# Two contraction blocks of three of the last output products moved into the last 20 attention steps, the last softmax sums inverted as columns, and one matmul pair reordered behind each head group

## The chip, the cores and the metric

One core of a Trainium2 chip runs the whole kernel. The metric is the device time of one execution in microseconds (us). Before the change it was 1708.81 us, the median of 3 runs (1708.61 to 1709.07).

## The reference

A transformer block with adaptive layer norm, on x of 2048 rows by 512, 32 heads of 16, and an inner width of 1792:

```python
mod = (silu(c) @ w_mod).reshape(1, 6, 1, -1)      # sa, ca, ga, sb, cb, gb
h = layernorm(x) * (1 + ca) + sa
q, k, v = split(h @ wqkv)                         # 32 heads of 16
o = softmax(q @ k.T * 16 ** -0.5) @ v
x = x + ga * (o @ wo)
h = layernorm(x) * (1 + cb) + sb
x = x + gb * (mish(h @ w1 + b1) @ w2)
```

## The kernel before

Everything is float32. Where a product must be precise and fast, each operand is split into a high part (fp32r, rounded) and a low part, and a product is three matmuls per contraction block of 128: high by high, high by low, low by high. `o_hl` holds the two parts of the attention output of one block of 512 queries, in four contraction blocks k of 128 features (k=0 to 3, eight heads each); the gate `ga` is already multiplied into `wo`.

The queries are cut into 4 blocks (NB) of 512, the heads into 8 groups of 4 (G), so there are 32 pairs of block and group, called n. Each n takes 16 steps; T = 512 steps, and t counts them. Step t works on one half s of the array's rows (rows 64 to 127 in even steps, 0 to 63 in odd ones). Its own work is in the list `mine`: 4 score products (`score`, L527: a matmul of 64 rows into a PSUM bank, then Exp on ScalarE) and, until 20 steps (PRO) before the end, up to 4 products for the row maxima of a later group (`max_tile`, L474: a matmul, then a reduction on VectorE). In the other half of the rows runs `part`, the piece of a background "unit" that this step takes: the MLP and the output projection of the block of queries before, each matmul cut into two halves of 64 rows, the lower half in the even step and the upper half in the odd step (`mm_half`, L131), both adding into one PSUM bank (`ms`). A unit of 12 matmuls takes four steps, six halves a step. `alone` holds maxima products that share the `part` side when `part` is short. At the end of the step comes `pv(t-2)` (L541), the four products of exponentials and values of two steps before, and after the last of a group `evac` (L557), in which ScalarE copies the finished group to `ot` (L563).

Two orderings matter here. First, when a new unit starts (`new`) the step emits one pair ahead of everything: the last own score and the last lone maximum ("early pair", L1230 to L1233), and only then the unit's first matmul, which needs the bank `ms` that ScalarE or VectorE may still be reading. Second, the two halves of the rows may not write one bank at the same time, so the first half-matmul of a step waits until ScalarE has done the exponential of the last score of the step before (`after`, L1226 and L1246); at a new unit this wait is dropped (L1139).

Scores and maxima take PSUM banks from a ring of 6 (`ring`, L150) in the order in which they are emitted: each needs the bank of the sixth before it to have been read.

The last block's own output projection and MLP run after the steps, in `tail` (L983). `tail_loads` (L977) fetches `wo` and the first weights 15 steps before the end; the rows of x to be added are fetched in `tail`. `wo_mms` (L998) makes the four output products, first contraction blocks 0 to 2 and then block 3, which needs the last group. `evac_last` (L605) normalises that group: one matmul with the 0/1 matrix `pick` lays the sums in rows 0 to 63 and the heads in rows 64 to 127 of one bank; VectorE inverts 64 by 512 sums, multiplies, and makes the two parts. Then come the additions to x, the layer norm, and held-back products of the block before (`held`), while TensorE keeps running. All this is one program order per engine, written out by this code.

Of the kernel before, what the change touches and what calls it, by code (L numbers as in the profile page):

```python
# [8 lines left out]
F32 = mybir.dt.float32  # L9
# [9 lines left out]
def adaln_block(ctx: ExitStack, tc: tile.TileContext, x, wqkv, wo, w1, b1, w2, c, w_mod, out):  # L19
    nc = tc.nc  # L20
    P = 128
    S, D = x.shape[1], x.shape[2]
    F = w1.shape[1]
    H = 32
    DH = D // H
    DK = D // P
    FT = F // P
    TB = 512
# [4 lines left out]
    T = 16 * NIT  # L33
# [3 lines left out]
    VROW = NKC * 4 * VW + 16  # L37
    LEAD = 4
    PRO = 16 + LEAD
# [6 lines left out]
    x = x[0]  # L46
# [11 lines left out]
    woscr = dram.tile([DK, P, 2, D], F32, name="woscr")  # L58
# [4 lines left out]
    ident = cst.tile([P, P], F32, name="ident")  # L63
# [20 lines left out]
    gates = [cst.tile([P, D], F32, name=f"gate{i}") for i in range(2)]  # L84
# [43 lines left out]
        acc, l, r, start, stop = m  # L128
        nc.tensor.matmul(acc, l, r, start=start, stop=stop)  # L129

    def mm_half(m, g, after):  # L131


        acc, l, r, start, stop = m
        i = nc.tensor.matmul(acc, l[64 * g:64 * g + 64], r[64 * g:64 * g + 64], start=start and not g, stop=bool(stop and g))  # L135
# [10 lines left out]
    NRING = 6  # L146
    ring_t = ps.tile([P, NRING, TB], F32, name="ring")
    ring_at = [0]

    def ring(w=1):  # L150
        if w == 2 and ring_at[0] % 2:
            ring_at[0] += 1
        b = ring_at[0] % NRING
        ring_at[0] += w
        return ring_t[:, b, :] if w == 1 else ring_t[:, b:b + 2, :]
# [41 lines left out]
    def at(h, f):  # L197

        hooks.setdefault(h, []).append(f)
# [4 lines left out]
    ka = [kq.tile([P, S], F32R, name=f"ka{i}") for i in range(2)]  # L204
# [116 lines left out]
    with ExitStack() as es:  # L321
# [276 lines left out]
    def make_pick():  # L598
# [3 lines left out]
        for i, src in enumerate((cols[:, :, DH:DH + 1].to_broadcast([P, 4, DH]), cols[:, :, :DH])):  # L602
            nc.gpsimd.tensor_copy(pick[:, i, :].rearrange("p (h w) -> p h w", w=DH), src)

    def evac_last(dn):  # L605

        ot, od, rb = mst["last"]
        oh, ol = o_hl[NB - 1]
        r = slice(64, P)
        nc.tensor.matmul(dn, mst["pick"].rearrange("p a w -> p (a w)"), ot, start=True, stop=True)  # L610
        nc.vector.reciprocal(rb[r], dn[:64, :])
        nc.vector.tensor_mul(od[r], dn[r, :], rb[r])
        hi_copy("v", oh[r, DK - 1, :], od[r])
        lo_sub("v", ol[r, DK - 1, :], od[r], oh[r, DK - 1, :])

# [351 lines left out]
    def half_tile(t, j, scr):  # L967

        w = t[:, j * 2 * D:(j + 1) * 2 * D]
        nc.sync.dma_start(w.bitcast(F32), scr.rearrange("p v m -> p (v m)"))  # L970
        return w.rearrange("p (v m) -> p v m", v=2)

    def w1_tail(f):
        i, j = divmod(f % 8, 2)
        return load_w1(f) if i == 1 else half_tile(ka[(1, 0, 2, 3)[i]], j, w1scr[f])

    def tail_loads():  # L977
        for k in range(DK):
            wos[k] = half_tile(ka[(4, 0)[k // 2]], k % 2, woscr[k])
        for f in range(2):  # L980
            w1s[f] = w1_tail(f)

    def tail():  # L983

# [2 lines left out]
        y, xn = [], []  # L987
        for v in (y, xn):
            for i in range(4):
                v.append(ap.tile([P, D], F32, tag=f"p{i}", name="y", bufs=3 + i % 2))  # L990
        for i in range(4):
# [6 lines left out]
        def wo_mms(i, ks):  # L998
            s = slice(i * P, (i + 1) * P)
            seq = [(l, r, k) for l, r in ((oh, 0), (oh, 1), (ol, 0)) for k in ks]  # L1000
            for j, (l, r, k) in enumerate(seq):
                nc.tensor.matmul(accs4[i], l[:, k, s], wos[k][:, r, :], start=(k == 0 and j == 0),
                                 stop=(k == 3 and j == 2))

        norms = []
        wo_mms(0, (0, 1, 2))
        evac_last(ring())
        wo_mms(1, (0, 1, 2))
        for i in (2, 3):
            accs4[i] = bank("ring")  # L1010
            wo_mms(i, (0, 1, 2))
        for i in range(4):
            wo_mms(i, (3,))
            nc.vector.tensor_add(y[i], accs4[i], y[i])
# [159 lines left out]
    def step(t):  # L1174
        second = t % 2
        n, u = t // 16, t % 16 // 2
        tm = t + PRO
        run_hooks(2 * t)
        if t < 0:

            for i in range(2):
                if tm < 16:
                    kb, jq = divmod(2 * tm + i, 8)
                else:
                    jq, kb = tm % 16 // 2, 2 * second + i
                max_pair(tm // 16, jq, kb)
            if second and tm % 16 == 15:
                neg_max(tm // 16)
            run_hooks(2 * t + 1)
            for f in ats.pop(t, []):  # L1190
                f()
            whole_units(2 * t + 1, CREDIT)
            do_specials(2 * t + 1)
            return
        s = 0 if second else 1
        own, others = ([score(n, j, v, 2 * u + i) for i in range(2) for j in range(2)] for v in (s, 1 - s))
        if not second and 1 < t < T:
            next_part(2 * t)
        part = list(cur["part"])
        f = len(part)  # L1200
        if t >= T:
            if t == T:
                cur["tag"] = "acc"
            run_hooks(2 * t + 1)
            pv(t - 2)
            whole_units(2 * t + 1, 8)
            do_specials(2 * t + 1)
            return
        if tm < T:
            o = max(0, (8 - f) // 2)  # L1210
            mo, alone = maxima(tm // 16, tm % 16 // 2, s, o)

            mine = [x for p in zip(mo, own) for x in p] + own[len(mo):]
        else:
            o = max(0, (4 - f) // 2)
            mine = own[o:] if second else own[:4 - o]
            alone = others[4 - o:] if second else others[:o]

            m = len(mine)
            if f > m:  # L1220
                mine = [mine[(i * m) // f] if (i + 1) * m // f > i * m // f else None for i in range(f)]
        beside = part + alone

        def emit(product):
            e = product()
            if e is not None and cur.pop("want", None):  # L1226
                cur["after"] = e

        mid = False
        if cur.pop("new", None) and alone and len(mine) > f:  # L1230

            emit(mine.pop())
            emit(beside.pop())  # L1233
        for i in range(max(len(mine), len(beside))):
            if i == len(mine) // 2:
                run_hooks(2 * t + 1)

            if not f and tm < T and i == (2 if mst.get("norming") else 3):
                pv(t - 2)
                mid = True  # L1240
            if i < f:
                last = i + 1 == f
                if i < len(mine) and mine[i] and not last:
                    emit(mine[i])
                for m in beside[i]:
                    mm_half(m, second, cur.pop("after", None))  # L1246
                if last:
                    cur["want"] = True
                    if i < len(mine):
                        emit(mine[i])  # L1250
                    if second and not cur["left"]:
                        cur["fin"](2 * t + 2)
                        cur["fin"] = None
            else:
                for x in (*mine[i:i + 1], *beside[i:i + 1]):
# [147 lines left out]
```

## Time and profile before

| | us |
|---|---|
| median of the runs | 1708.81 |
| the profiled execution | 1705.6 |
| its span (first to last instruction) | 1703.8 |
| the last 19 steps (from 1548.82 until the last values products at 1598.19) | 49.37 |
| the last three values products | 2.71 |
| `tail` until output block 3 can start | 9.34 |
| from there to the end | 93.56 |

The profiled execution took 1.8 us more than its span, and the median of the runs is 3.2 us above it. A timeline row gives the start in us from the beginning of the span, the length in us, the engine, the line in the listing, the operation, the tile written and the tiles read, the shape, and how many instructions were merged; in brackets is the idle time before it and what ended that. A window row gives a stretch, its length, and for each engine the busy time and number of instructions in it, then the granted TensorE clock, the DMA share and GB/s. A float32 matmul shows as two instructions. Busy rows of TensorE overlap, since matmuls are pipelined: what counts is the distance from one start to the next.

### The profile page before, as it was taken

The page shows a single profiled execution, that of the slowest core. Times are in us where ns is not written, and L with a number is a line of the kernel's source. Part 1 is how long each engine was busy: PE and PEld are TensorE (multiplying, and loading weights), DVE is VectorE, ACT ScalarE, POOL GpSimd, SP SyncE. Part 2 cuts the span into 40 slices and gives each one's busy share as a digit, 9 for nine tenths or more (in the row PEclk, how much of TensorE's full clock was granted, in tenths as well). Part 3 has the DMA queues.
Part 4 walks back from the last instruction along what each step waited for, and adds up shares of the span by engine and source line. Part 5 has one row for each costly group of instructions (what it writes and reads, how often), then busy time and mean ns, then how long its engine had stood idle before and what let it go on. Part 6 is the DMA issues. An engine that isn't in the chain of part 4 may idle for free.

```text
span 1703.8 us, 33660 instructions
## 1 busy us (share of the span) xinstructions
PE 1675.0 (98%) x12372; PEld 915.5 (54%) x12372; DVE 1437.6 (84%) x2368; ACT 1356.9 (80%) x2613; POOL 807.6 (47%) x829
## 2 busy tenths in 40 slices
PE   7999999999999999999999999999999999999999
PEld 5755665555445455555555455555545445554587
DVE  6888888888889888888889898888889888883377
ACT  6257777777778988888888998888878988888574
POOL 5155224665413464655423564556323654555442
PEclk9999999999999999999999999999999999999999
DMA  7777457777773342434355433424354433424261
GB/s 253 187 235 214 109 162 216 237 234 222 234 208 101 99 109 76 134 80 126 83 151 148 118 74 94 139 76 126 88 143 124 124 93 83 137 68 157 84 228 63
DMA packets 113997, 240.08 MB, mean 141 GB/s; under 512 B 24048, under 2 KB 49648, under 8 KB 107784
## 3 DMA queue, kind: packets, MB, share of 16 engines
q1 hardware_dynamic: 113832, 237.92, 48.6%
q8 instruction: 98, 1.61, 0.4%
q14 instruction: 67, 0.55, 0.1%
HBM read 179.95 MB, written 51.44 MB: 136 GB/s over the span
## 4 chain that ended last, share of the span: by engine, by line
PE 84%; DMA 5%; ACT 4%; DVE 4%; issue 1%; SPq 0%; POOL 0%; ACTq 0%; DVEq 0%; POOLq 0%
PE bk L549 26%; PE ring L531 20%; PE ring L482 18%; PE bk L135 10%; PE bk L129 4%; DVE mx L484 3%; ACT pr L534 3%; PE ring L1110 2%; PE ring L129 2%; DMA qa<-mt 1%; DMA ka<-kscr 1%; PE ring L496 1%; DMA w<-woscr 1%; ACT hb L722 1%; PE ring L843 0%
## 5 line engine op out<-in xcount | busy, mean ns | idle before, releaser
L484 DVE TENSOR_REDUCE mx<-ring 128x1 f32<-128x512 f32 x1968 | 1222.0, 681 | 159.9 <-PE ring L482 142.1
L534 ACT ACTIVATE pr<-ring 128x512 f32<-128x512 f32 x2048 | 1078.2, 602 | 217.8 <-PE bk L135 128.1
L482 PE MATMUL ring<-ka,qa 64*128 64x512 f32 x1968 | 815.7, 429 | 5.2 <-ACT pr L534 3.5
L531 PE MATMUL ring<-qa,ka 64*128 64x512 f32 x2048 | 759.2, 403 | 6.5 <-DMA qa<-mt 3.7
L549 PE MATMUL bk<-pr,vg 128*32 128x512 f32 x4096 | 545.1, 604 | 0.0
L482 PEld LDWEIGHTS ring<-ka,qa 64*128 64x128 f32 x1968 | 349.1, 184 | 321.6 <-DVE mx L484 230.2
L531 PEld LDWEIGHTS ring<-qa,ka 64*128 64x128 f32 x2048 | 373.5, 184 | 200.2 <-DVE mx L484 129.8
L135 PE MATMUL bk<-h,w 64*128 64x512 f32 (+1 forms) x1080 | 279.6, 391 | 0.1
L135 PE MATMUL bk<-w,a_h 64*128 64x512 f32 x632 | 211.6, 413 | 0.3 <-ACT pr L534 0.2
L135 PEld LDWEIGHTS bk<-h,w 64*128 64x128 f32 x1080 | 178.5, 184 | 13.0 <-ACT pr L534 4.3
L549 PEld LDWEIGHTS bk<-pr,vg 128*32 128x32 f32 x4096 | 80.8, 108 | 137.7 <-issue 126.4
L135 PE MATMUL bk<-w,a_l 64*128 64x512 f32 x316 | 124.0, 392 | 0.0
L135 PEld LDWEIGHTS bk<-w,a_h 64*128 64x128 f32 x632 | 107.5, 184 | 16.9 <-ACT pr L534 8.3
L899 POOL TENSOR_TENSOR y<-yd,y 128x512 f32<-128x512 f32 x44 | 56.8, 1292 | 90.5 <-ACT yd L898 85.3
L734 POOL TENSOR_SCALAR qq<-ee 128x512 f32<-128x512 f32 x25 | 15.5, 619 | 171.5 <-ACT ee L728 171.5
L750 POOL TENSOR_TENSOR qq<-qq,rr 128x512 f32<-128x512 f32 x42 | 54.2, 1289 | 83.8 <-ACT rr L744 83.6
L736 POOL TENSOR_TENSOR hb<-hb,ee 128x512 f32<-128x512 f32 x42 | 54.1, 1287 | 82.7 <-DVE ee L732 80.7
L135 PE MATMUL bk<-w,o_hl 64*128 64x512 f32 x288 | 79.2, 404 | 0.0
L98 POOL TENSOR_TENSOR a_l<-hb,a_h 128x512 fp32r<-128x512 f32 x53 | 72.0, 1358 | 4.4
L135 PEld LDWEIGHTS bk<-w,a_l 64*128 64x128 f32 x316 | 58.3, 184 | 4.9
L135 PE MATMUL bk<-h_h,wl 64*128 64x512 f32 x168 | 57.1, 420 | 0.0
L752 POOL TENSOR_TENSOR rr<-rr,qq 128x512 f32<-128x512 f32 x42 | 54.1, 1287 | 3.5
(189 smaller groups left out, 1841.5 us busy)
## 6 DMA issues: line engine op xcount, KB each, us to landing
ka<-kscr SPq DMA_DIRECT2D x124, 384.0 KB
w<-w2scr SPq DMA_DIRECT2D x56, 512.0 KB
w<-w1scr SPq DMA_DIRECT2D x46, 512.0 KB
vg<-vscr SPq DMA_DIRECT2D x32, 552.0 KB
qa<-qscr SPq DMA_DIRECT2D x124, 100.0 KB
kscr<-qh SPq DMA_DIRECT2D x16, 512.0 KB
qscr<-qh SPq DMA_DIRECT2D x32, 256.0 KB
hl<-in_B_w SPq DMA_DIRECT2D x28, 256.0 KB
```

Source lines behind the costliest of these rows:

```text
L98: (nc.gpsimd if eng == "p" else nc.vector).tensor_sub(lo, src, hi.bitcast(F32))
L129: nc.tensor.matmul(acc, l, r, start=start, stop=stop)
L135: i = nc.tensor.matmul(acc, l[64 * g:64 * g + 64], r[64 * g:64 * g + 64], start=start and not g, stop=bool(stop and g))
L482: nc.tensor.matmul(pm, qt[64 * s:64 * s + 64, qs * P:(qs + 1) * P], kt[64 * s:64 * s + 64, kb * TB:(kb + 1) * TB], start=True, stop=True)
L484: nc.vector.tensor_reduce(out=mxs[n][:, s, 4 * j + qs, kb:kb + 1], in_=pm, op=ALU.max, axis=AX.X)
L531: nc.tensor.matmul(p_, kt[64 * s:64 * s + 64, kc * P:(kc + 1) * P], qt[64 * s:64 * s + 64, :], start=True, stop=True)
L534: e = nc.scalar.activation(pr, p_, AF.Exp, scale=SCALE)
L549: nc.tensor.matmul(accs[n][32 * h:32 * h + 32, :], vgs[n][:, o:o + 32], pts.pop((t, h)), start=(kc == 0), stop=(kc == 15))
L736: (nc.vector if tail else nc.gpsimd).tensor_mul(hb, hb, ee)
L750: nc.gpsimd.tensor_mul(qq, qq, rr)
L752: nc.gpsimd.tensor_mul(rr, rr, qq)
L899: nc.gpsimd.tensor_add(y[i], yd, y[i])
```

## The change

1. In the steps t = 494 to 511, two more half-matmuls go into `mine` of each step, at its third and fifth place (`first_part`): the six matmuls of contraction blocks 0 and 1 for the first three of the four output products, so 18 matmuls, each as two halves, an upper half in the even step and a lower half in the odd step. They add up in the ring's sixth bank, which is taken out of the ring from step 492 (`kept`); every sixth step VectorE adds the bank to the rows of x in `ys`. `tail` then multiplies block 2 alone for these three products. While such a product is unfinished, a new unit keeps the wait on the exponential.
2. Loads move: two blocks of `wo` to step 483 and two row tiles of x to step 484, ahead in the sync engine's queue of a w1 load, the transfers of a group's sums, the last values load, three w2 loads and the row maxima's transfers; the third row tile of x moves to step 500. The row tiles lie in the gates' buffers and in a free values buffer.
3. The last group's sums: four matmuls of `ot` with four columns of the identity give them as 128 by 16, VectorE inverts these and copies them out to 128 by 256, the heads come with the `pick` matmul and are copied by ScalarE, and four matmuls with the identity turn the inverses back into rows 64 to 127, by which VectorE multiplies.
4. There is no early pair in the steps t with t % 16 = 2. The unit's first matmul then follows the first of `mine`, and the last score and the lone maximum come at the end of the step. This applies to 18 steps: 18, 34, 130, 162 to 274 (every 16th), 386 to 482 (every 16th).

```diff
     def ring(w=1):
         if w == 2 and ring_at[0] % 2:
+            ring_at[0] += 1
+        if kept and ring_at[0] % NRING == NRING - 1:
             ring_at[0] += 1
...
+    def sums_last(cs):
+        ot = mst["last"][0]
+        for q in range(4):
+            nc.tensor.matmul(cs[:, 4 * q:4 * q + 4], ot[:, q * P:(q + 1) * P], ident[:, DH::32], start=True, stop=True)
+        rc = ap.tile([P, 16], F32, tag="rc", name="rc", bufs=2)
+        nc.vector.reciprocal(rc, cs[:, :16])
+        wide = ap.tile([P, TB], F32, tag="p0", name="wide", bufs=3)[:, :256].rearrange("p (q h d) -> p q h d", q=4, h=4)
+        mst["rc"] = wide
+        nc.vector.tensor_copy(wide, rc.rearrange("p (q h) -> p q h", h=4)[:, :, :, None].to_broadcast([P, 4, 4, DH]))
+
+    def heads_last(dn):
+        ot, od, _ = mst["last"]
+        nc.tensor.matmul(dn, mst["pick"].rearrange("p a w -> p (a w)"), ot, start=True, stop=True)
+        nc.scalar.copy(od[64:], dn[64:, :])
+
     def evac_last(dn):
-        ot, od, rb = mst["last"]
+        od, rc = mst["last"][1], mst["rc"]
...
-        nc.tensor.matmul(dn, mst["pick"].rearrange("p a w -> p (a w)"), ot, start=True, stop=True)
-        nc.vector.reciprocal(rb[r], dn[:64, :])
-        nc.vector.tensor_mul(od[r], dn[r, :], rb[r])
+        for q in range(4):
+            nc.tensor.matmul(dn[64:, q * P:(q + 1) * P], rc[:, q].rearrange("p h w -> p (h w)"), ident, start=True, stop=True)
+        nc.vector.tensor_mul(od[r], dn[r, :], od[r])
...
+    def first_part(h):
+        u = first_of
+        if not u["left"] and u["next"] < FIRST:
+            i = u["next"]
+            u["next"] += 1
+            oh, ol = o_hl[last]
+            acc = ring_t[:, NRING - 1, :]
+            s = slice(i * P, (i + 1) * P)
+            seq = [(l[:, k, s], wos[k][:, v, :]) for l, v in ((oh, 0), (oh, 1), (ol, 0)) for k in range(2)]
+            u["left"] = [[(acc, l, r, j == 0, j == len(seq) - 1)] for j, (l, r) in enumerate(seq)]
+            u["fin"] = lambda: nc.vector.tensor_add(ys[i], acc, ys[i])
+        u["part"], u["left"] = u["left"][:2], u["left"][2:]
...
-        wo_mms(0, (0, 1, 2))
+        kept.clear()
+        wo_mms(0, (2,))
+        sums_last(ring())
+        heads_last(ring())
         evac_last(ring())
-        wo_mms(1, (0, 1, 2))
+        wo_mms(1, (2,))
         for i in (2, 3):
             accs4[i] = bank("ring")
-            wo_mms(i, (0, 1, 2))
+            wo_mms(i, (2,) if i < FIRST else (0, 1, 2))
...
-            cur.pop("after", None)
+            if not first_of["left"]:
+                cur.pop("after", None)
...
+            if first_of["part"]:
...
+                for i, slot in enumerate(first_of["part"]):
+                    mine.insert(2 + 2 * i, lambda slot=slot: [mm_half(m, 1 - second, None, second) for m in slot] and None)
...
-        if cur.pop("new", None) and alone and len(mine) > f:
+        if cur.pop("new", None) and alone and len(mine) > f and t % 16 != 2:
             emit(mine.pop())
             emit(beside.pop())
...
+        if second and first_of["part"] and not first_of["left"]:
+            first_of["fin"]()
...
+    at(2 * (T - 29), lambda: load_wos((0, 1)))
+    at(2 * (T - 28), lambda: load_ys((0, 1)))
+    at(2 * (T - 12), lambda: load_ys((2,)))
     at(2 * T - 30, tail_loads)
```

More of the change, by code (lines that the diff above doesn't have):

```diff
@@ L129, in mm_go, with mm_half @@
         nc.tensor.matmul(acc, l, r, start=start, stop=stop)
-    def mm_half(m, g, after):
+    def mm_half(m, g, after, then=None):
         acc, l, r, start, stop = m
-        i = nc.tensor.matmul(acc, l[64 * g:64 * g + 64], r[64 * g:64 * g + 64], start=start and not g, stop=bool(stop and g))
+        then = g if then is None else then
+        i = nc.tensor.matmul(acc, l[64 * g:64 * g + 64], r[64 * g:64 * g + 64], start=start and not then, stop=bool(stop and then))
         if after is not None:
@@ L148, in adaln_block @@
     ring_at = [0]
+    kept = []
     def ring(w=1):
         if w == 2 and ring_at[0] % 2:
+            ring_at[0] += 1
+        if kept and ring_at[0] % NRING == NRING - 1:
             ring_at[0] += 1
@@ L975, in w1_tail, with load_wos, load_ys @@
         return load_w1(f) if i == 1 else half_tile(ka[(1, 0, 2, 3)[i]], j, w1scr[f])
+    FIRST = 3
+    first_of = {"left": [], "fin": None, "part": [], "next": 0}
+    ys = {}
+    def load_wos(ks):
+        for k in ks:
+            wos[k] = half_tile(ka[(4, 0)[k // 2]], k % 2, woscr[k])
+    def load_ys(js):
+        for i in js:
+            ys[i] = gates[i] if i < 2 else ap.tile([P, VROW], F32, tag="vg", name="vg", bufs=2)[:, :D]
+            r = 4 * last + i
+            nc.sync.dma_start(ys[i], x[r * P:(r + 1) * P, :])
     def tail_loads():
-        for k in range(DK):
-            wos[k] = half_tile(ka[(4, 0)[k // 2]], k % 2, woscr[k])
+        load_wos((2, 3))
         for f in range(2):
             w1s[f] = w1_tail(f)
+    def first_part(h):
[10 more added lines that the diff above has]
+        u["part"], u["left"] = u["left"][:2], u["left"][2:]
     def tail():
@@ L989, in tail @@
             for i in range(4):
-                v.append(ap.tile([P, D], F32, tag=f"p{i}", name="y", bufs=3 + i % 2))
-        for i in range(4):
+                v.append(ys[i] if v is y and i < FIRST else ap.tile([P, D], F32, tag=f"p{i}", name="y", bufs=3 + i % 2))
+        for i in range(FIRST, 4):
             r = 4 * last + i
@@ L1001, in wo_mms @@
             for j, (l, r, k) in enumerate(seq):
-                nc.tensor.matmul(accs4[i], l[:, k, s], wos[k][:, r, :], start=(k == 0 and j == 0),
+                nc.tensor.matmul(accs4[i], l[:, k, s], wos[k][:, r, :], start=(k != 3 and j == 0),
                                  stop=(k == 3 and j == 2))
         norms = []
-        wo_mms(0, (0, 1, 2))
+        kept.clear()
+        wo_mms(0, (2,))
+        sums_last(ring())
+        heads_last(ring())
         evac_last(ring())
-        wo_mms(1, (0, 1, 2))
+        wo_mms(1, (2,))
         for i in (2, 3):
             accs4[i] = bank("ring")
-            wo_mms(i, (0, 1, 2))
+            wo_mms(i, (2,) if i < FIRST else (0, 1, 2))
         for i in range(4):
@@ L1199, in step @@
         part = list(cur["part"])
+        if not second:
+            first_of["part"] = []
+            if t == T - PRO:
+                kept.append(NRING - 1)
+            elif T - PRO < t < T:
+                first_part(2 * t)
         f = len(part)
@@ L1217, in step @@
             alone = others[4 - o:] if second else others[:o]
+            if first_of["part"]:
+                assert f
+                for i, slot in enumerate(first_of["part"]):
+                    mine.insert(2 + 2 * i, lambda slot=slot: [mm_half(m, 1 - second, None, second) for m in slot] and None)
             m = len(mine)
```

## The prediction

> **What bounds the kernel now.** I read the page first: the share of each engine, then the chain of work that ended last.
>
> ```profile
> span 1703.8 us, 33660 instructions
> PE 1675.0 (98%) x12372; PEld 915.5 (54%) x12372; DVE 1437.6 (84%) x2368; ACT 1356.9 (80%) x2613; POOL 807.6 (47%) x829
> PE 84%; DMA 5%; ACT 4%; DVE 4%; issue 1%; SPq 0%; POOL 0%; ACTq 0%; DVEq 0%; POOLq 0%
> ```
>
> TensorE sets the time over nearly the whole span, so an edit counts by the distance between TensorE's starts that it removes or adds. Three places are touched: the 18 steps that lose their early pair, the last 20 steps, and the tail. Their stretches, cut by windows (columns: length; PE, PEld, DVE, ACT, POOL busy), first the last steps, the tail up to output block 3, and what follows:
>
> ```profile
> 1548.82:1598.19 49.37, 48.98 (x335) 22.75 (x334) 5.46 (x9) 43.53 (x85) 28.06 (x27) 1.00 0.27 92
> 1600.90:1610.24 9.34, 9.34 (x43) 7.26 (x39) 5.16 (x4) 0.59 (x1) 0.00 (x0) 1.00 0.91 336
> 1610.24:1640.00 29.76, 29.76 (x162) 25.50 (x161) 20.46 (x32) 18.32 (x30) 11.42 (x20) 1.00 0.62 238
> ```
>
> TensorE is never idle in the tail, so matmuls taken out of it shorten it one for one, as long as nothing else becomes late. Then the 18 steps, each from one values product's start to the next: one of the usual kind, the mildest, the one with the most in it, and the sum over all 18. Below them step 322, at the same place in its group but in the middle of a unit and so without an early pair, and the sum over the 18 steps that follow the 18.
>
> ```profile
> 628.01:631.27 3.26, 3.09 (x23) 1.34 (x22) 2.81 (x5) 3.26 (x8) 2.80 (x3) 1.00 0.88 194
> 1377.98:1380.98 3.00, 3.00 (x25) 1.33 (x23) 2.75 (x6) 3.00 (x7) 1.29 (x1) 1.00 0.01 3
> 1279.58:1283.38 3.80, 3.61 (x28) 2.04 (x26) 3.80 (x8) 3.48 (x7) 0.29 (x1) 1.00 0.05 7
> sum 59.48, PE 56.36 PEld 26.20 DVE 52.77 ACT 59.01 POOL 18.66; mean PE 3.13 PEld 1.46 DVE 2.93 ACT 3.28 POOL 1.04
> 1003.57:1006.40 2.83, 2.83 (x24) 1.52 (x23) 2.47 (x5) 2.67 (x7) 2.67 (x3) 1.00 0.12 17
> sum 51.51, PE 51.51 PEld 28.35 DVE 39.73 ACT 40.71 POOL 19.17; mean PE 2.86 PEld 1.57 DVE 2.21 ACT 2.26 POOL 1.06
> ```
>
> The 18 steps average 59.48 / 18 = 3.30 us, the step without an early pair 2.83: the excess is 18 x 0.47 = 8.5 us. ScalarE is busy for 59.0 of the 59.5 us there, but only 40.7 of 51.5 in the steps after, so it catches up at once.
>
> **The early pair: what the stall is.** One of the 18, step 178, in the timeline, TensorE and then ScalarE:
>
> ```profile
> 629.01 0.72 PE L482 MATMUL ring<-ka,qa 64*128 64x512 f32 x2
> 629.35 0.39 PE L135 MATMUL bk<-w,a_h 64*128 64x512 f32 x1
> ...
> 630.05 0.39 PE L135 MATMUL bk<-w,a_h 64*128 64x512 f32 x1
> ...
> 630.61 0.50 PE L482 MATMUL ring<-ka,qa 64*128 64x512 f32 x1 [0.17 <-ACT pr L534]
> ...
> 631.27 0.64 PE L549 MATMUL bk<-pr,vg 128*32 128x512 f32 x4
> ...
> 628.40 0.68 ACT L722 ACTIVATE hb<-bk,b1c 128x512 f32<-128x512 f32 x1
> 628.97 0.60 ACT L534 ACTIVATE pr<-ring 128x512 f32<-128x512 f32 x1
> 629.45 0.61 ACT L563 COPY ot<-bk 128x512 f32<-128x512 f32 x1
> 629.91 1.62 ACT L534 ACTIVATE pr<-ring 128x512 f32<-128x512 f32 x3
> ```
>
> In these steps ScalarE takes the unit's bank (L722, or a copy) and `ot` between two steps' exponentials. The early score's exponential can therefore start only at 629.91 and is over at about 630.55 (it is the first of three that overlap in 1.62). The ring has six banks, so the sixth product after the early score, the third maximum, needs its bank: it should start at 630.28, one slot of 0.23 us after 630.05, and starts at 630.61. With the restart (0.33 us to the next start, as from 629.01 to 629.35, instead of 0.23) the step loses 0.42 us against 2.84.
>
> Without the early pair all products of the step stand two places earlier in the ring. The third maximum then needs the bank of the last step's final score, read by 629.57: no wait. Two waits are left. The unit's first matmul comes in the first slot, 629.01, and needs the bank that L722 reads until 629.08: about 0.13 us with the semaphore. The lone maximum in the last slot, about 630.63, needs the first score's exponential, which now starts no earlier than 629.91 and ends near 630.63: about 0.05. So step 178 would come to 3.02 and gain 0.24. The same working by each step's own rows: 13 of the 18 gain 0.24 to 0.32, in sum 3.4; three mild ones like 1377.98 gain 0.11 each, 0.3. In the last two, the one at 1279.58 and one like it, transposes of the layer norm make the step long, and the copy that the unit waits for is VectorE's and late, which the early pair had covered: I put them at -0.2 together. Sum 3.5 us. Bounds: nothing, if the stall returns at the unit's first matmul; all of the excess, 8.5 less 0.9 for the two steps' transposes (two times four at 0.11, below), 7.6, if all 18 fall to 2.84. A value below the middle is right because the waits that remain are ScalarE's, whose work is not less.
>
> **The tail.** TensorE, then VectorE's chain for the last group, with ScalarE's copy that starts it:
>
> ```profile
> 1600.90 2.36 PE L1002 MATMUL bk<-ka,o_hl 128*128 128x512 f32 x9
> 1603.10 1.02 PE L610 MATMUL ring<-ot,pick 128*128 128x512 f32 x2
> 1603.56 2.66 PE L1002 MATMUL bk<-ka,o_hl 128*128 128x512 f32 x9
> 1606.05 4.35 PE L1002 MATMUL ring<-ka,o_hl 128*128 128x512 f32 x18
> ...
> 1604.16 3.35 DVE L611 RECIPROCAL rb<-ring 64x512 f32<-64x512 f32 x1 [5.10 <-PE ring L610]
> 1607.55 0.69 DVE L612 TENSOR_TENSOR od<-ring,rb 64x512 f32<-64x512 f32 x1
> 1608.28 0.42 DVE L93 CAST o_hl<-od 64x512 fp32r<-64x512 f32 x1
> 1608.73 0.69 DVE L98 TENSOR_TENSOR o_hl<-od,o_hl 64x512 fp32r<-64x512 f32 x1
> ...
> 1601.04 0.59 ACT L563 COPY ot<-bk 128x512 f32<-128x512 f32 x1 [1.77 <-PE bk L549]
> ```
>
> Of 36 matmuls before output block 3, 18 go: the x18 row takes 1610.24 - 1606.05 = 4.19 us, 0.233 each, so 4.19 us less. What is added has no row here; the nearest are
>
> ```profile
> 1603.26 0.86 PE ring L610 x2
> 1617.35 0.87 PE ring L1035 x8
> ...
> L399 PE MATMUL bk<-sel,row 128*128 128x1 f32 x16 | 3.6, 353 | 0.0
> L584 DVE RECIPROCAL rc<-sm 128x16 f32<-128x16 f32 x31 | 7.5, 241 | 0.0
> ```
>
> from the chain of waits and the groups by shape. Turning the inverses back is four float32 products of 128 columns, together as many columns as the one L610: 0.86. The four for the sums are eight instructions that load 128 weights each, like the transposes of L1035 (0.87 for 8): 0.87, where L399, with one column each, shows that few columns don't make them much cheaper. Bounds for the two: 0.4 each (one pass instead of two) and 1.4 to 2.8 each if each instruction takes the 0.18 to 0.35 us of L399's rows, which ran in the first 15 us. Two changes of the array's shape, into 64 columns and back, cost a restart each: 0.1 (0.33 instead of 0.23, as above). So the stretch becomes 9.34 - 4.19 + 0.86 + 0.87 + 0.2 = 7.1, 2.2 us less; by the bounds, between 3.4 less and 0.5 more, and I keep 2.2, since the added products use the same operands as L610 and L1035.
>
> What could be late instead: the sums start when `ot` is there (1601.7), by then three matmuls are done (1601.6). Sums until 1602.6, inversion 0.24, copy to 256 columns about 0.4 (half of a 0.69 row), ready at 1603.4, when TensorE has finished the `pick` product. Products with the identity until 1604.4, then 0.69, 0.42 and 0.69 on VectorE: both parts at 1606.4. TensorE reaches output block 3 at 1608.0, so 1.6 us of other output products cover it; ScalarE's copy of the heads (0.6) ends 1604.2. Everything behind block 3 follows in the same order, fully busy, and moves with it.
>
> A rule that speaks against the added products: the Trainium skill, "TensorEngine Tiling (Array Packing)", section Key Properties, says that a change of tiling mode drains TensorE. The first slot after each values product, 0.33 instead of 0.23, agrees with a small drain, and the sum has it. The same page, Instruction Overhead, gives about 60 cycles to a matmul of few columns, by which (an estimate) the sums would take 0.2 us and the total be 0.7 us better; the rows of L399 do not look like that.
>
> **The last 20 steps.** Two steps, TensorE at the values products and at their ends, then ScalarE:
>
> ```profile
> 1571.76 1.06 PE L549 MATMUL bk<-pr,vg 128*32 128x512 f32 x8
> 1572.75 0.49 PE L135 MATMUL bk<-w,a_h 64*128 64x512 f32 x1
> ...
> 1574.34 1.06 PE L549 MATMUL bk<-pr,vg 128*32 128x512 f32 x8
> 1575.41 0.50 PE L135 MATMUL bk<-w,a_h 64*128 64x512 f32 x1
> ...
> 1573.29 2.06 ACT L534 ACTIVATE pr<-ring 128x512 f32<-128x512 f32 x4 [0.44 <-PE ring L531]
> 1582.56 0.69 DVE L898 COPY yd<-bk 128x512 f32<-128x512 f32 x1 [3.15 <-PE bk L135]
> ```
>
> A step has six half-matmuls of the unit in one half of the rows, and four scores in the other: two slots are free. The two new halves fill them, and I cost them at nothing; the cover is the unit's six slots of 0.23. Without it, 36 x 0.233 = 8.4 us. The fifth bank is enough: a score then needs the fifth before it, whose exponential (four in 2.06 us, done at 1575.35, before the next step starts) is always over. The wait kept at new units costs 1.07 - 0.99 = 0.08, in three steps (498, 502, 510): 0.2. VectorE's addition (0.69) stands behind a unit's copy at one place only, from 1582.56 to about 1583.95, just when the next product wants the bank: 0.1. Against this, the first score now stands ahead of the waiting matmul and starts its exponential up to 0.08 earlier; I take 0.1. Sum: +0.2, from -0.5 to +8.4. The moved loads are seven issues on a queue that has time (DMA share 0.27 above), at least four steps ahead of the sums' transfers behind them: nothing.
>
> **Sum.** -3.5 - 2.2 + 0.2 = -5.5. The span 1703.8 becomes 1698.3, the profiled run 1705.6 becomes 1700.1, and the median, 3.2 above the profiled run, 1708.8 - 5.5 = 1703.3.
>
> **The rivals.**
> - The stall only moves: the unit's first matmul, or the next step, takes what the third maximum lost, since ScalarE's work in the 18 steps is not less (59.0 of 59.5). Against it: 40.7 of 51.5 in the step after. Only the tail is left: -2.0, 1706.8.
> - All 18 steps return to 2.84, since a step without early pair does so although it has `ot` too. For it the 2.83 row; against it that row has one ScalarE instruction less (x7). -7.6 - 2.0: 1699.2.
> - The small products cost more, and with them TensorE waits for VectorE: 1.5 us more in the tail, -4.0: 1704.8.
> - Slower: the new halves are not covered, because both halves of the rows cannot run full with three accumulating banks. Place: the 18 steps from 494; price up to 8.4, -5.7 + 8.4: 1711.5; it decides from 5.7 us, two thirds of the halves, on. Against it: ordinary steps run eight slots with both halves full at 0.23 a slot.
>
> **How the numbers follow.** A change under 0.2% (3.4 us, beyond 1705.4 to 1712.2) cannot be told from none. Forecast 0.55, all returned 0.1, dearer products 0.1: these are faster, and so 0.75. The moved stall 0.17 is within, and most of the slower case (0.08): 0.21 within, 0.04 slower. The range takes in the moved stall and nearly all of the other gain: 1699.6 to 1707.0.
>
> **What would show it.** Right: L482's waits for ScalarE gone from the 18 steps, their sum near 56; the last steps' stretch still near 49.4; output block 3 7.1 us after the last values product; VectorE's inversion at 0.24. Wrong: the sum still near 59, a first matmul of a unit that starts 0.3 late, last steps over 2.7 each, or TensorE idle before block 3.

## The result, and the profile after

The changed kernel takes 1701.47 us (median of 8 runs, 1698.15 to 1704.48) against 1708.09 for the kernel before (median of 8, 1704.94 to 1709.07; the three runs told at the start are among them). The ratio is 0.9965, with a 95% interval from 0.9954 to 0.9976: 4.1 to 7.9 us faster. The page of the kernel after:

```profile
span 1702.7 us, 33730 instructions
PE 1674.4 (98%) x12406; PEld 921.7 (54%) x12406; DVE 1438.2 (84%) x2372; ACT 1359.4 (80%) x2614; POOL 809.3 (48%) x829
PE 90%; DVE 3%; DMA 3%; ACT 2%; issue 1%; SPq 0%; POOL 0%; ACTq 0%; DVEq 0%; POOLq 0%
```

TensorE still sets the time (busy for 98% of the span, 90% of the chain of work that ended last). The span is only 1.1 us shorter than before: the profiled execution is the slowest of the eight (1704.48, 3.0 above their median), and that of before (1705.6) is 2.5 below its median. So the stages have to be read one by one. In the windows of the kernel after, the last steps and the tail, cut at the same instructions as before:

```profile
1550.08:1599.01 48.93, 48.93 (x371) 25.03 (x370) 6.75 (x11) 43.33 (x85) 28.18 (x27) 1.00 0.24 77
1601.73:1609.07 7.34, 7.34 (x41) 5.45 (x38) 2.36 (x5) 1.17 (x2) 0.00 (x0) 1.00 0.93 340
```

and the 18 steps without their early pair: step 178, the sum over the 18, and the sum over the 18 steps behind them:

```profile
631.70:634.73 3.03, 3.03 (x24) 1.81 (x23) 2.61 (x5) 3.03 (x8) 2.85 (x3) 1.00 0.90 196
sum 55.90, PE 55.45 PEld 32.49 DVE 49.80 ACT 55.15 POOL 18.13; mean PE 3.08 PEld 1.81 DVE 2.77 ACT 3.06 POOL 1.01
sum 51.45, PE 51.45 PEld 28.39 DVE 42.69 ACT 45.04 POOL 18.45; mean PE 2.86 PEld 1.58 DVE 2.37 ACT 2.50 POOL 1.03
```

The 18 steps went from 59.48 to 55.90 (3.6 us), the tail from 9.34 to 7.34 (2.0), the last steps from 49.37 to 48.93 (0.4): 6.0 us together. The steps behind the 18 did not grow (51.51 before). From 1609.07 to the end of the span it is 93.6 us, as before.

Some 4.9 us of this are missing from the profiled span. Most of them lie in the first third, where TensorE waits for transfers. Six steps there, 80, 81, 96, 112, 132 and 133, in the windows before, their sum:

```profile
sum 21.84, PE 17.50 PEld 9.01 DVE 14.99 ACT 14.95 POOL 11.51; mean PE 2.92 PEld 1.50 DVE 2.50 ACT 2.49 POOL 1.92
```

and after, with the steps 80, 81 and 133 by themselves:

```profile
337.27:342.76 5.49, 3.51 (x23) 1.78 (x22) 3.02 (x6) 3.17 (x7) 4.31 (x5) 0.87 0.84 245
342.76:346.57 3.81, 3.81 (x24) 1.67 (x22) 1.94 (x4) 1.67 (x4) 3.56 (x5) 0.74 0.93 206
...
496.12:500.04 3.92, 3.92 (x24) 1.77 (x22) 1.86 (x5) 1.67 (x4) 0.00 (x0) 0.71 0.09 12
sum 26.10, PE 21.03 PEld 9.88 DVE 15.05 ACT 15.38 POOL 14.42; mean PE 3.50 PEld 1.65 DVE 2.51 ACT 2.56 POOL 2.40
```

26.10 - 21.84 = 4.3 us. The third number from the end of a row is the granted clock: it fell to 0.71 to 0.87 in these rows. Over the profiles of all the kernels below, the same six steps take 19.5 to 26.1 us, whichever part of the change is in (23.2 for the kernel after once more, e11_after_again), and two others, 108 and 128, vary by 4.3 and 1.4 us. So this changes from execution to execution, and the spans of single profiles can't be compared as they stand.

**What the changed step looks like.** Step 178 after, TensorE, then ScalarE, in the timeline:

```profile
632.70 0.50 PE L487 MATMUL ring<-ka,qa 64*128 64x512 f32 x1
632.83 0.49 PE L136 MATMUL bk<-w,a_h 64*128 64x512 f32 x1
...
633.51 0.39 PE L536 MATMUL ring<-qa,ka 64*128 64x512 f32 x1
...
633.74 0.38 PE L487 MATMUL ring<-ka,qa 64*128 64x512 f32 x1
...
634.32 0.47 PE L487 MATMUL ring<-ka,qa 64*128 64x512 f32 x1
634.73 0.64 PE L554 MATMUL bk<-pr,vg 128*32 128x512 f32 x4
...
632.08 0.69 ACT L744 ACTIVATE hb<-bk,b1c 128x512 f32<-128x512 f32 x1
```

The unit's first matmul waits 0.13 us for L744's bank (632.83 instead of 632.70), the third maximum comes a slot of 0.23 behind the product before it (633.74), the lone maximum last (634.32), and the step ends 3.03 us after it began.

**What the new tail looks like.** TensorE and VectorE between the last group's `ot` and both parts of it:

```profile
1602.54 1.02 PE L614 MATMUL ring<-ident,ot 128*128 128x4 f32 x8
...
1603.42 1.10 PE L624 MATMUL ring<-ot,pick 128*128 128x512 f32 x2
1603.65 0.26 DVE L616 RECIPROCAL rc<-ring 128x16 f32<-128x16 f32 x1 [3.17 <-issue]
1603.94 0.29 DVE L619 COPY wide<-rc 128x256 f32<-128x256 f32 x1
...
1604.45 1.09 PE L633 MATMUL ring<-ident,wide 128*64 128x128 f32 x8
...
1605.47 0.97 PE L1051 MATMUL bk<-ka,o_hl 128*128 128x512 f32 x3
...
1606.82 0.69 DVE L98 TENSOR_TENSOR o_hl<-od,o_hl 64x512 fp32r<-64x512 f32 x1
```

From start to start the sums take 1603.42 - 1602.54 = 0.88 us, the heads 1.03, the inverses turned back 1605.47 - 1604.45 = 1.02. Both parts are there at 1607.51, and TensorE reaches output block 3 at 1609.07 without having stood still.

### The profile page after: what moved, and what is told of

It is laid out like the page before. It is cut to its first block, busy times and chain, and to the rows that moved or that the text cites. A ratio compares the mean times of both kernels' runs of the same rounds, so it can differ in the third digit from the quotient of the medians.

```text
span 1702.7 us, 33730 instructions
## 1 busy us (share of the span) xinstructions
PE 1674.4 (98%) x12406; PEld 921.7 (54%) x12406; DVE 1438.2 (84%) x2372; ACT 1359.4 (80%) x2614; POOL 809.3 (48%) x829
## 4 chain that ended last, share of the span: by engine, by line
PE 90%; DVE 3%; DMA 3%; ACT 2%; issue 1%; SPq 0%; POOL 0%; ACTq 0%; DVEq 0%; POOLq 0%
PE bk L554 28%; PE ring L536 22%; PE ring L487 19%; PE bk L136 10%; PE bk L129 3%; PE ring L1162 2%; PE ring L129 2%; DVE mx L489 2%; ACT pr L539 1%; DMA qa<-mt 1%; DMA xt<-in_A_x 1%; PE ring L501 1%; DMA w<-w1scr 1%; DMA w<-woscr 1%; PE ring L865 0%
```

## The experiments

All times are us. "18 steps" is their sum; "493 to 510" the stretch between the starts of two values products, without the last of the steps; "to block 3" is from the last values product to the start of output block 3, and beside it how long block 3 takes. These four are from the trace of each kernel. The first row is the profile of before.

| kernel | ratio to before (95%) | 18 steps | 493 to 510 | to block 3, block 3 |
|---|---|---|---|---|
| before | 1 | 59.48 | 47.92 | 9.33, 2.78 |
| after | 0.9965 (0.9954 to 0.9976) | 55.89 | 47.56 | 7.34, 2.78 |
| e1_pair_only | 0.9978 (0.9968 to 0.9988) | 55.97 | 47.92 | 9.33, 2.78 |
| e2_columns_only | 1.0013 (1.0002 to 1.0024) | 59.43 | 47.92 | 11.45, 2.77 |
| e3_rows | 0.9958 (0.9944 to 0.9973) | 55.97 | 47.54 | 6.58, 3.18 |
| e4_no_halves | 0.9964 (0.9948 to 0.9980) | 55.88 | 47.48 | 7.34, 2.78 |
| e5_two_maxima | 1.0002 (0.9992 to 1.0011) | 60.93 | 47.53 | 7.33, 2.80 |
| e6_two_maxima_all | 1.0267 (1.0253 to 1.0280) | 60.70 | 47.55 | 7.33, 2.80 |
| e7_rows_low_last | 0.9962 (0.9950 to 0.9974) | 55.88 | 47.55 | 6.58, 2.86 |
| e8_four_banks | one run, 1700.78 | 55.95 | 47.43 | 7.33, 2.80 |
| e9_no_pair | 0.9983 (0.9971 to 0.9995) | 55.75 | 47.55 | 7.34, 2.78 |
| e10_pair_where_it_helps | 0.9970 (0.9957 to 0.9983) | 55.76 | 47.83 | 6.58, 2.87 |
| e11_after_again | 0.9966 (0.9955 to 0.9978) | 55.91 | 47.55 | 7.33, 2.80 |

**The pair alone** (e1_pair_only: the kernel before with this one line of the change):

```diff
-        if cur.pop("new", None) and alone and len(mine) > f:
+        if cur.pop("new", None) and alone and len(mine) > f and t % 16 != 2:
```

> The kernel before with one edit: no early pair in the 18 steps with t % 16 = 2. My theory: the stall at the third maximum is the early score's ring bank, so the 18 steps alone come to 55.9 us in sum (59.5 before), everything else stays, and the time is 3.6 us below the kernel before. Rival one: the shortening of those steps needs the rest of the change or is given back in the steps behind, then the sum or the steps behind stay as they were in total and the time is that of the kernel before (0 +- 1). Rival two: the tail carries the whole 6 us, with the same reading.

The median was 1703.64 against 1707.32, 3.7 us. In its windows the sums over the 18 steps and over the 18 behind them are

```profile
sum 55.98, PE 55.53 PEld 32.61 DVE 49.91 ACT 55.25 POOL 18.04; mean PE 3.09 PEld 1.81 DVE 2.77 ACT 3.07 POOL 1.00
sum 51.52, PE 51.52 PEld 28.39 DVE 42.63 ACT 44.99 POOL 18.44; mean PE 2.86 PEld 1.58 DVE 2.37 ACT 2.50 POOL 1.02
```

so the line is worth 3.5 us by itself, and nothing of it comes back in the steps behind: ScalarE's busy time there rose from 40.7 to 45.0 of 51.5, into time that it had free.

**The columns alone** (e2_columns_only: the kernel before with part 3 of the change, the last group's sums inverted as columns, and all 36 matmuls still ahead of block 3):

```diff
...
+        sums_last(ring())
+        heads_last(ring())
         evac_last(ring())
```

> The kernel before with the last sums inverted as columns and nothing else. My theory: TensorE is never idle there, so the eight small products are paid in full (0.9 and 1.0 us): output block 3 starts 11.3 us after the last values product instead of 9.34, and the time is 2.0 us above the kernel before, although VectorE's inversion falls from 3.35 to 0.26 us. Rival: block 3 waits for VectorE's chain, then the shorter inversion pays for the products, the stretch is 9.3 or less and the time 0 to 1 us below.

```profile
1606.20:1617.65 11.45, 11.45 (x59) 8.93 (x55) 2.36 (x5) 1.17 (x2) 0.00 (x0) 1.00 0.81 299
```

TensorE is busy all of it, and it is 2.1 us longer than before's 9.34: the columns cost TensorE 2.1 us, and save VectorE 2.8 (5.16 busy before, 2.36 here) that no one waits for in this arrangement. By the ratio the whole kernel is 2.2 us slower than before (0.3 to 4.1).

**The halves with the old inversion** (e3_rows: the kernel after with `evac_last` of the kernel before):

```diff
...
-        sums_last(ring())
-        heads_last(ring())
         evac_last(ring())
```

> The changed kernel with the inversion in rows as before (one product with pick, 64 by 512 inverted). Rival, by which the columns are needed: with 18 matmuls gone TensorE waits for the inversion in rows longer than the columns cost, and block 3 starts later than the 7.34 us of the changed kernel (8 or more). My theory: the pick product ends 1.7 us after the last values product, the inversion (3.35), the product (0.69) and the high part (0.42) end at 6.3, the low part at 7.0; TensorE, done at 5.1, waits about 1.2 us for the high part and 0.2 for the low one, so block 3 is through 0.5 to 0.9 us earlier than in the changed kernel, and the time is 0.5 to 0.9 us lower.

The windows until block 3 starts, and of block 3:

```profile
1600.23:1606.81 6.58, 5.39 (x24) 3.63 (x21) 4.54 (x4) 0.59 (x1) 0.00 (x0) 1.00 0.92 322
1606.81:1609.99 3.18, 3.11 (x12) 2.26 (x13) 2.45 (x5) 0.00 (x0) 0.17 (x1) 1.00 0.40 162
```

and VectorE's chain:

```profile
1602.17 3.35 DVE L616 RECIPROCAL rb<-ring 64x512 f32<-64x512 f32 x1 [3.19 <-PE ring L615]
...
1606.28 0.42 DVE L93 CAST o_hl<-od 64x512 fp32r<-64x512 f32 x1
1606.74 0.69 DVE L98 TENSOR_TENSOR o_hl<-od,o_hl 64x512 fp32r<-64x512 f32 x1
```

Now TensorE does wait (5.39 busy of 6.58), until the high part is there at 1606.70, and block 3 takes 0.4 longer because its third matmul needs the low part, ready at 1607.43. Even so block 3 ends 9.76 after the last values product instead of 10.12. The waits, 1.2 us before block 3 and 0.4 in it, are cheaper than the 2.1 us of products that avoid them.

**The same, with the low parts last** (e7_rows_low_last: e3_rows, and in block 3 the high terms of the first two output products ahead of the first low term):

```diff
...
+        wo_high(0)
+        wo_high(1)
         for i in range(4):
-            wo_mms(i, (3,))
+            if i > 1:
+                wo_high(i)
+            wo_low(i)
             nc.vector.tensor_add(y[i], accs4[i], y[i])
```

> The changed kernel with the inversion in rows, and in output block 3 the high terms of the first two products ahead of their low terms. Theory: in the kernel with rows alone block 3 starts 6.58 us after the last values product but takes 3.18 instead of 2.78, since the low part comes 0.7 us after the high one; with the low terms later it takes 2.78 again, so the end of block 3 is at 9.36 instead of 9.76 (10.12 in the changed kernel): 0.4 us below the kernel with rows, 0.8 below the changed kernel. Rival: the later end of the first product makes the layer norm late, and TensorE waits at the transposes by the same 0.4.

```profile
1602.85:1605.71 2.86, 2.86 (x13) 2.33 (x13) 2.01 (x3) 0.00 (x0) 0.00 (x0) 1.00 0.49 196
```

Block 3 starts after 6.58 as in e3_rows, is back at 2.86 and ends 9.44 after the last values product, 0.7 us earlier than in the kernel after. No kernel here has a shorter tail; the medians (1699.92 against 1707.37 for before) can't tell it from the kernel after.

**Are the new halves free?** (e4_no_halves: the kernel after without them, but with their places in the order.)

```diff
-                mine.insert(2 + 2 * i, lambda slot=slot: [mm_half(m, 1 - second, None, second) for m in slot] and None)
+                mine.insert(2 + 2 * i, None)
```

> The changed kernel without the 36 half-matmuls of the last 20 steps: contraction blocks 0 and 1 of three output products are not computed; bank, waits, loads and additions stay. My theory: the halves run in free slots of the other half of the rows and cost nothing: the stretch of steps 493 to 511 is the same within 0.2 us, and so is the time. Rival: they cost part of their 8.4 us (0.233 each), then the stretch is shorter here by 1 to 8 us.

The steps 493 to 510 take 47.48 without the halves and 47.56 with them: 36 half-matmuls for 0.1 us, against 8.4 without cover.

**Is the fifth bank needed?** (e8_four_banks: the kernel after with two banks kept out of the ring in the last 20 steps.)

```diff
-        if kept and ring_at[0] % NRING == NRING - 1:
-            ring_at[0] += 1
+        if kept and ring_at[0] % NRING >= NRING - 2:
+            ring_at[0] += NRING - ring_at[0] % NRING
```

> The changed kernel with two banks out of the ring in the last 20 steps, so that four are left for the scores. Theory: a score then needs the bank of the score four before it, whose exponential is over at least 0.6 us earlier, so steps 493 to 510 take 47.6 us as with five banks (within 0.2). Rival: the sixth bank already cost something, then a second one costs visibly, 1 us or more in these steps.

47.43 in its one execution: four banks are enough, so five were no limit.

**Another pair behind a group** (e5_two_maxima: the kernel after, with an early pair in the 18 steps that has two maxima, the first own one and the lone one; e6_two_maxima_all: such a pair at every new unit):

```diff
-        if cur.pop("new", None) and alone and len(mine) > f and t % 16 != 2:
-            emit(mine.pop())
+        if cur.pop("new", None) and alone and len(mine) > f:
+            emit(mine.pop(0 if t % 16 == 2 else -1))
```

> The changed kernel, but behind a group there is an early pair again, made of two maxima (the first own one and the lone one) in place of the last score and the lone maximum. My theory: the stall came from which product was early, not from a pair being early: a maximum's bank is read by VectorE, which has no copy of the group to make, so no bank is late; and the pair covers the wait of the unit's first matmul (0.13) that the changed kernel still has. The 18 steps fall from 55.9 to about 52.5 us in sum (16 times 2.84 and two of 3.5) and the time by 3.4 us below the changed kernel. Rival: any pair ahead of the unit delays what follows in the ring; then the sum is 56 or more and the time is that of the changed kernel or above it.

> As in the kernel with two maxima behind a group, but for every new unit. My theory: in the other steps ScalarE has no copy of a group, so the early score's exponential is in time in most of them and the order matters little: 0 to 3 us less than with the two maxima behind a group alone. Rival: the score is emitted early to start ScalarE's exponentials sooner, and without it ScalarE is late in the 118 other steps: above that kernel by 1 us or more.

The 18 steps did not get shorter but longer, 60.9, and in e6 the 123 other steps with a new unit went from 371.0 to 417.2. Step 178 of e5_two_maxima, TensorE, then VectorE:

```profile
634.13 0.50 PE L487 MATMUL ring<-ka,qa 64*128 64x512 f32 x2
...
636.01 0.50 PE L536 MATMUL ring<-qa,ka 64*128 64x512 f32 x1
...
634.67 2.48 DVE L489 TENSOR_REDUCE mx<-ring 128x1 f32<-128x512 f32 x4 [0.41 <-PE ring L487]
```

VectorE reduces one maximum in 2.48 / 4 = 0.62 us, and has read the second of the pair at 634.67 + 1.24 = 635.91. The eighth product in the ring, the last score, needs that bank, the sixth before it, and starts at 636.01. The theory that a pair without a score would not stall has fallen. Step 186 of e6_two_maxima_all shows the same (3.29 us instead of 2.84; VectorE has read the second maximum at 671.92, the last score starts at 672.02), so there too the late engine is VectorE, and not ScalarE as the rival had it. What the early pair does wrong is the same in both forms: its two products go to the front of the ring, and when the engine that reads one of them is late (ScalarE with `ot` before, VectorE with two reductions in a row here), a product at the end of the step waits for the bank.

**No pair anywhere** (e9_no_pair: the condition of the change set so that no step has one):

> The kernel after, with no early pair at any new unit (the 123 other steps that still have one lose it too). Theory (the pair stalls only where ScalarE copies `ot` between two steps; elsewhere it covers the unit's wait for its bank at no cost): without the pair the unit's first matmul waits some 0.07 to 0.13 us as in step 178 of the kernel after, so the 123 steps, 371.0 us in sum and 2.84 in the median, come to 2.91 to 2.97, 9 to 16 us more; ratio to before 1.001 to 1.006. Rival one (the wait is hidden anyway): sum 371, ratio 0.996. Rival two (the pair itself costs 0.2 wherever it stands, as it did in the 18 steps): the sum falls by 123 x 0.2 = 25 us, ratio 0.982.

The ratio is 0.9983, some 3 us above after's, though the two intervals just overlap. Steps 186 and 296 in the windows of the kernel after, then of e9_no_pair:

```profile
654.63:657.47 2.84, 2.84 (x24) 1.35 (x23) 2.40 (x5) 2.84 (x7) 0.00 (x0) 1.00 0.64 233
976.01:979.16 3.15, 3.09 (x24) 1.32 (x22) 2.90 (x6) 3.15 (x7) 1.05 (x1) 1.00 0.67 195
```

```profile
650.50:653.45 2.95, 2.95 (x23) 1.75 (x22) 2.54 (x5) 2.74 (x7) 0.00 (x0) 1.00 0.67 236
972.61:975.44 2.83, 2.83 (x24) 1.52 (x22) 2.60 (x6) 2.83 (x6) 0.91 (x1) 1.00 0.59 187
```

Of the 119 steps (123 without 80, 96, 112 and 132, which wait for transfers), 57 became longer, 5.1 us in sum, like step 186, 15 shorter, 2.6 us in sum, like step 296, and the others stayed. In the 119 steps the pair is thus worth 2.6 us; the sum over all 123 stayed (369.8), because the four that wait for transfers fell by 3.8. The theory's sign was right and its size too large: in about half of the steps nothing is late at the unit's bank, and the 15 shorter ones show that the pair stalls in some steps without the copy of `ot` too.

**The pair only where it helps** (e10_pair_where_it_helps, with the kernel after once more on the same chip, e11_after_again):

```diff
-        if cur.pop("new", None) and alone and len(mine) > f and t % 16 != 2:
+        if cur.pop("new", None) and alone and len(mine) > f and t % 16 != 2 and t not in NO_PAIR:
```

> The kernel of e7_rows_low_last, with the early pair also left out in 11 further steps, those in which e9_no_pair was shorter by 0.1 us or more (150, 158, 166, 280, 288, 292, 296, 380, 410, 422, 426). Theory (each step's stall is its own, and does not move): the 11 steps shorten by the same 2.2 us, the others stay; ratio to before 0.995 against 0.996 of the kernel after. Rival (what they gain in e9 came from the steps without pair around them): nothing, ratio as after's.

> The kernel after once more, on the same chip as e10_pair_where_it_helps, so that the two can be set side by side: 0.9965 as before; the further edits of e7 and e10, 0.7 and 2.2 us, would put e10 2 to 3 us below it.

1702.48 against 1701.13: no gain, as the rival had it, though not for its reason. The 11 steps did shorten by 2.2 us in sum (37.72 to 35.51), but it came back in other steps. Steps 426 and 428 in the windows of e7_rows_low_last, then of e10_pair_where_it_helps:

```profile
1349.37:1352.64 3.27, 3.10 (x25) 1.32 (x23) 3.01 (x6) 3.27 (x7) 1.06 (x1) 1.00 0.71 246
...
1355.86:1359.58 3.72, 3.34 (x23) 1.40 (x23) 3.69 (x8) 3.33 (x6) 3.55 (x4) 1.00 0.00 0
```

```profile
1354.71:1357.56 2.85, 2.85 (x25) 1.57 (x23) 2.63 (x6) 2.85 (x6) 0.82 (x1) 1.00 0.78 210
...
1360.72:1364.75 4.03, 3.42 (x24) 1.40 (x23) 4.00 (x8) 3.28 (x7) 3.86 (x4) 1.00 0.00 0
```

Step 426 gains 0.42 and step 428 loses 0.31, with VectorE busy for 4.00 of its 4.03 us, unlike in the steps behind the 18. In 168, 295, 298 and 428, all at most three steps behind one of the 11, TensorE now waits 0.10 to 0.23 us for a reduction of VectorE, which is busy through nearly all of each. The up to four steps behind each of the 11 give back 1.2 us; the steps 399, 437 and 502, further off, grew by 0.8 in sum, and why stays open. Over all steps but those around waits for transfers the two profiles differ by 0.2 us. In these two cases, a stall that was removed beside a busy engine moved for the larger part, and beside a free one it went away.

## Why the prediction was right

- **The early pair, -3.5:** 59.48 to 55.90, -3.6, and -3.5 with nothing else changed. Step 178 was put at 3.02 and came to 3.03, with the wait at the unit's first matmul that was named, 0.13. The mild ones (18, 34, 434) gained 0.14 to 0.17 where 0.11 was put, the two with transposes (274, 402) stood still where a loss of 0.2 was put; the 13 others gained 3.2 where 3.4 was put.
- **That the stall would not move:** the 18 steps behind are 51.45 (51.51 before). The reason given, ScalarE's free time there, fits e1, where its busy time rose by 4.3 us and the steps did not grow. e10 shows the other case.
- **The tail, -2.2:** -2.0. The term that was small is the added products. The sums were right (0.88 against 0.87). The inverses took 1.02 where 0.86 was put, and the `pick` product kept TensorE for 1.03 instead of 0.86: 0.33 more in the two, against the 0.2 put for the two changes of shape. Weight loading sets the sums' pace: 8 instructions of 4 columns in 0.88 us, 0.11 each, and their 8 weight loads run without a gap, from 1602.50 to 1603.47. So the rule of the Trainium skill, "TensorEngine Tiling (Array Packing)", Instruction Overhead, by which (an estimate) they would have taken 0.2 us, does not hold for these float32 products, each of which has a weight load of its own. VectorE's inversion took 0.26 (0.24 put), its copy 0.29 (0.4 put). The bound of 0.5 more does not come out of the prices beside it: 2.8 each and 0.2 for the restarts, less 4.19, make 1.6 more. Both parts came 1.6 us ahead of block 3, as forecast, though 5.8 us after the last values product where 5.5 was put.
- **What the prediction didn't see:** that this cover was too dear. It costed the columns as part of the tail's sum, -4.19 + 1.93, and asked only what could be late with them. It did not work out the tail without them, which e3 and e7 show to be 0.4 and 0.7 us shorter.
- **The last steps, +0.2:** -0.4. The halves are free, as put. The kept wait came as put: the steps 498, 502 and 510 grew by 0.24 in sum (0.2 put). VectorE's addition cost 0.05 (step 506; 0.1 put). The term that was mis-sized, so that the sum failed in sign, is the earlier start of the first score, 0.1 in all: the other 14 steps became shorter by 0.7 in sum. Step 504 shows how. In the timeline before, TensorE and then ScalarE, the first half-matmul waits for the last exponential of the step before, over at 1578.07, and the first score starts with it, 1.13 after the values product (1577.00):

```profile
1578.13 0.50 PE L135 MATMUL bk<-w,a_h 64*128 64x512 f32 x1
1578.13 0.49 PE L531 MATMUL ring<-qa,ka 64*128 64x512 f32 x1
...
1576.01 2.06 ACT L534 ACTIVATE pr<-ring 128x512 f32<-128x512 f32 x4
...
1578.67 2.07 ACT L534 ACTIVATE pr<-ring 128x512 f32<-128x512 f32 x4
```

and after, the score goes ahead, 1.00 behind the values product (1577.96):

```profile
1578.96 0.50 PE L536 MATMUL ring<-qa,ka 64*128 64x512 f32 x1
1579.08 0.50 PE L136 MATMUL bk<-w,a_h 64*128 64x512 f32 x1
...
1579.50 2.08 ACT L539 ACTIVATE pr<-ring 128x512 f32<-128x512 f32 x4
```

ScalarE's four exponentials then start 1.54 instead of 1.67 behind the values product, and the next step's first half-matmul 1.00 instead of 1.07 behind its own. Before, the first score started at 1.07 to 1.23 in 13 of the 18 steps; after, it starts at 1.00 in all of them. The 0.4 is there with the halves left out as well (47.92 to 47.48 in e4), so it is not the halves' but comes with their places in the order. That the earlier score is the whole of it was not tried by itself. Nor were the moved loads; from 1515 us to output block 3 TensorE waits for no transfer in the kernel after.
- **The total:** -5.5 put; the stages add up to -6.0, the medians differ by 6.6. That 1701.47 is 1.8 below the 1703.3 predicted comes from the median of before being 0.7 lower over eight runs than over three, the last steps' 0.6, and the runs' spread.

## What to carry to other kernels

Before an edit at a stall, look at how busy the engines that read the ring are in the neighbouring steps: with free time there the gain stayed (3.5 of 3.5 us here), without it the gain was lost in other steps (2.2 of 2.2). In a ring of buffers a product moved to the front brings its reader's lateness to a product a whole ring later; look there, not beside it. And when work is taken off the engine that bounds a stage, price again the work that had been added to cover it: here 2.1 us of products covered waits of 1.2 and 0.4 us.

## What the runs showed of the hardware

TensorE's clock fell after waits for transfers, and not after each. In the timeline before, step 80 waits, and the clock stays at 1.00:

```profile
339.87 0.47 PE L531 MATMUL ring<-qa,ka 64*128 64x512 f32 x1 [1.37 <-DMA qa<-mt]
```

In the timeline after, the same step:

```profile
340.32 0.46 PE L536 MATMUL ring<-qa,ka 64*128 64x512 f32 x1 [1.98 <-DMA qa<-mt]
...
341.71 0.62 PE L487 MATMUL ring<-ka,qa 64*128 64x512 f32 x1
342.14 0.62 PE L536 MATMUL ring<-qa,ka 64*128 64x512 f32 x1
342.76 1.93 PE L554 MATMUL bk<-pr,vg 128*32 128x512 f32 x8
```

From about 341.4 a slot takes 0.43 us instead of 0.23, and the values products 1.93 instead of 1.06, until 344.7: some 3.3 us at about half the rate, which adds 1 us and more to the wait itself. After a wait of 1.26 us in step 132 the same happened (step 133 above: 3.92 instead of 2.90, clock 0.71). In e4_no_halves the clock stayed at 1.00 although no matmul started for 2.59 us in step 80, against 2.57 us in the kernel after. The Trainium skill, "TensorE: Matmul & The Clock Gate", Part 1, says that the array runs at half clock after an idle window of some 3.4 us, and that the windows run freely. The half rate and the length of the dip agree; that waits of 1.3 to 2 us are enough, and only sometimes, is more than it states. A freely running window may be why it depends on where the wait falls, but no run here shows that.
